# Moving one working tile behind the others, and the sums and x pieces of a three-stage network on one Trainium2 core

## The chip, the cores and the metric

The kernel runs on one core of one Trainium2 chip. The metric is the time of one execution on the device, in microseconds, as the median of several runs. TensorE (PE, with its weight loads PEld) multiplies out of SBUF into PSUM, VectorE (DVE), ScalarE (ACT) and GpSimd (POOL) work on SBUF and PSUM, and SyncE (SP) issues nearly all DMAs, in the order in which they are written.

## What is computed

Pooled attention over four batches of 576 tokens and eight heads makes x of 2304 x 512; a dense mixture of four experts follows, and a gated network with two more matrices. Everything is float32.

```python
k_p = k.reshape(B, H, Sp, 8, D).mean(axis=3)          # v_p likewise; Sp = 72
attn = softmax(q @ k_p.T / 8); x = attn @ v_p         # then laid out as 2304 x 512

p = domain_probs / (domain_probs.sum(-1, keepdims=True) + 1e-09)
for e in range(4):                                    # w1[e]: 512 x 1024, w2[e]: 1024 x 512
    out += p[:, e:e+1] * (np.maximum(x @ w1[e], 0.0) @ w2[e])

a = x @ w1; b = x @ w2                                # 512 x 1024 each
h = a * b @ w3                                        # 1024 x 1024
return h @ w_out                                      # 1024 x 512
```

## The kernel before

**Precision.** Every large product runs in the 4-byte type float32r, those of the attention stage in float32. An operand is split into a high part (a ScalarE copy) and a low part (the difference, by VectorE or GpSimd), `hi_lo`, lines 176 to 178; `mm3`, lines 171 to 174, issues three matmuls for one product: high x low, low x high, high x high. Each matmul brings its own weight load of 128 x 128 values; the moving operand has 384 or 512 columns.

**Order.** The whole program is written by hand in the order in which each engine runs it. The stages are: attention for six blocks of 384 tokens, woven into expert 0; experts 1 to 3 in batches of 768 tokens (`batch`, three batches an expert); w3 times w_out, folded into one matrix (`w3_h`, units "w"); the gated network in two halves of three batches each (from line 1329).

**A batch of 768 tokens.** The first layer of experts 1 to 3 and of the gated stage goes by `seven`: four rounds j, each with seven products of 2 x 3 matmuls of 384 columns, thus 168 matmuls (tile "s"). VectorE adds the seven results up (line 952) into the tiles x, u, v and c. The second layer of an expert then takes 6 token tiles x 8 x 3 = 144 matmuls of 512 columns (tile "g"), in the gated stage 6 x 4 x 3 = 72. Banks of PSUM go round in a ring of eight (`bank_r`). During an expert's second layer, the dictionary `acts` puts other work at numbered places, one place for each three matmuls.

**Sums.** What the experts add up lies in DRAM (`acc_d`). `load_ob(m)` (line 1182) fetches the sum of one token tile, and `give(m)` adds the expert's part (line 1242) and stores it or, for the last expert, turns it. In an expert's last batch the six sums lie at places that `ob_place` names: rows 2 and 3 of "plain", a place in x5l, then rows 0, 1 and 2 of "plain", fetched at places 14, 15, 16, 33, 34 and 40. Rows 0 and 1 of "plain" also hold the sums of the next expert's weights (`weights_of`, places 5 to 23).

**Rounding.** The 8-byte inputs of the gated network are brought to 4 bytes by `Rounding.step`, five VectorE operations and one GpSimd operation (lines 284 to 290), with three places for incoming data ("din", in x5h); a step fetches the data of the steps that follow (`load`), up to `most` steps in all.

**x for the gated stage.** Its seven products need x, its high and low parts, and four sums of them. `load_x` (line 774) fetches a half of x for the next batch, `prepare_x` makes the parts. The first operand (kc = 0) goes in three lumps behind the products j = 0, 1 and 2, the second one (kc = 1) in one lump behind the fourth product. Results of the second layer go out of PSUM by ScalarE (line 1395) into one of the four tiles of `rawpool` and are stored (line 1396). x's parts are stored too, for the second half (`put_away`, line 913).

**Places in SBUF.** Four pools follow each other: const, w2pool (the split w2 tiles, later w34), rawpool, and home. In the built program w2pool begins at byte 17,024 = 133 x 128, and home at 57,984 = 453 x 128. In home come first "plain", then "round" (the hidden values z and, later, w_out, called wo), "ap1" (later "xo", the x operands) and twelve tiles of 6,144 bytes (the split weights wh, wl, wx, z7 and others). All are multiples of 128 bytes but one:

```python
    WORK = 320
    PLAIN = WORK + XT + 3072          # XT = 6144: 9,536 bytes = 74.5 x 128
    plain = area("plain", PLAIN, F32, "plain")
    round_ = area("round", (FC - 1) * ZT + 2 * EXTRA, F32R, "round")
```

So every tile of home behind "plain" starts 64 bytes past a multiple of 128, and w2pool's tiles start at one. The matmuls of an expert's second layer read w2 as the moving operand (w2pool) and z as the stationary one (home); those of `seven` read xo and the split weights, both in home; those with wo read wo and w3, both in home.

## Time and profile before

| | |
|---|---|
| median of 3 runs | 1180.4 us (1179.27 to 1181.14) |
| the profiled execution's own time | 1179.82 us |
| its span, first to last instruction | 1177.7 us |
| PE busy | 1155.6 us, 98% of the span |
| DVE, POOL, ACT busy | 800.6, 421.0, 369.6 us |
| DMA | 213.85 MB, mean share of the 16 engines 59% |

A matmul's end is modelled and matmuls overlap, so PE's busy time tells whether it stands still, not how fast it goes. The pace is read from the starts of matmuls that follow each other, or from a stretch of known content divided by its number of matmuls.

### The profile page before, as it was taken

The page shows a single profiled execution, that of the slowest core. Times are in us where ns is not written, and L with a number is a line of the kernel's source. Part 1 is how long each engine was busy: PE and PEld are TensorE (multiplying, and loading weights), DVE is VectorE, ACT ScalarE, POOL GpSimd, SP SyncE. Part 2 cuts the span into 40 slices and gives each one's busy share as a digit, 9 for nine tenths or more (in the row PEclk, how much of TensorE's full clock was granted, in tenths as well). Part 3 has the DMA queues.
Part 4 walks back from the last instruction along what each step waited for, and adds up shares of the span by engine and source line. Part 5 has one row for each costly group of instructions (what it writes and reads, how often), then busy time and mean ns, then how long its engine had stood idle before and what let it go on. Part 6 is the DMA issues. An engine that isn't in the chain of part 4 may idle for free.

```text
span 1177.7 us, 17100 instructions
## 1 busy us (share of the span) xinstructions
PE 1155.6 (98%) x5966; PEld 1033.6 (88%) x5966; DVE 800.6 (68%) x1464; ACT 369.6 (31%) x615; POOL 421.0 (36%) x393
## 2 busy tenths in 40 slices
PE   8999999999999999999999899999999999999998
PEld 6788888989889898889898798989889898998997
DVE  6866553577768696658679486967677766774554
ACT  4543442344313152404134241405343313230100
POOL 6965213333525166534436371515000111331211
PEclk9999999999999999999999999999999999999999
DMA  8956514364966636295944568784476064946341
GB/s 210 212 145 142 168 68 161 147 208 166 312 220 205 213 85 191 82 312 168 269 148 131 176 201 201 215 225 119 157 180 251 28 268 171 337 166 253 130 167 54
DMA packets 213766, 213.85 MB, mean 182 GB/s; under 512 B 88880, under 2 KB 169008, under 8 KB 213680
## 3 DMA queue, kind: packets, MB, share of 16 engines
q1 hardware_dynamic: 213392, 212.23, 58.1%
q8 instruction: 47, 0.77, 0.3%
q10 hardware_dynamic: 288, 0.52, 0.1%
q14 instruction: 39, 0.32, 0.1%
HBM read 140.87 MB, written 71.83 MB: 181 GB/s over the span
## 4 chain that ended last, share of the span: by engine, by line
PE 76%; DVE 9%; issue 6%; DMA 4%; POOL 3%; ACT 1%; SPq 1%; POOLq 0%; DVEq 0%; ACTq 0%
PE g L173 15%; PE g L172 14%; PE g L174 14%; PE s L172 9%; PE s L174 9%; PE s L173 9%; PE x_ps L556 1%; PE sc L502 1%; DVE wl L178 1%; DVE plain L952 1%; PE at_ps L541 1%; DMA raw<-in_moe_w_dram 1%; POOL round L178 1%; POOL w2l L178 1%; DMA acc<-plain 1%
## 5 line engine op out<-in xcount | busy, mean ns | idle before, releaser
L172 PE MATMUL s<-xo,wh 128*128 128x384 f32 x624 | 209.7, 336 | 7.1 <-DVE plain L1242 7.1
L178 POOL TENSOR_TENSOR round<-x5l,round 128x768 fp32r<-128x768 f32 x60 | 112.2, 1871 | 278.2 <-ACT round L177 259.3
L952 DVE TENSOR_TENSOR plain<-s,plain 128x384 f32<-128x384 f32 x300 | 157.9, 554 | 78.2 <-ACT plain L956 37.6
L174 PE MATMUL s<-xo,wh 128*128 128x384 f32 x624 | 209.2, 335 | 0.0
L173 PE MATMUL s<-xo,wl 128*128 128x384 f32 x624 | 209.2, 335 | 0.0
L172 PE MATMUL g<-w2l,round 128*128 128x512 f32 x522 | 207.3, 397 | 0.0
L173 PE MATMUL g<-w2h,round 128*128 128x512 f32 x522 | 206.6, 396 | 0.0
L174 PE MATMUL g<-w2h,round 128*128 128x512 f32 x522 | 206.2, 395 | 0.0
L172 PEld LDWEIGHTS s<-xo,wh 128*128 128x128 f32 x624 | 117.7, 189 | 9.3 <-issue 4.6
L174 PEld LDWEIGHTS g<-w2h,round 128*128 128x128 f32 x522 | 98.1, 188 | 23.3
L173 PEld LDWEIGHTS s<-xo,wl 128*128 128x128 f32 x624 | 117.6, 188 | 0.6
L174 PEld LDWEIGHTS s<-xo,wh 128*128 128x128 f32 x624 | 117.6, 188 | 0.0
L172 PEld LDWEIGHTS g<-w2l,round 128*128 128x128 f32 x522 | 98.2, 188 | 21.8 <-issue 0.8
L173 PEld LDWEIGHTS g<-w2h,round 128*128 128x128 f32 x522 | 98.1, 188 | 21.3
L956 ACT ACTIVATE plain<-s 128x384 f32<-128x384 f32 x60 | 29.1, 484 | 258.0 <-PE s L174 232.3
L290 POOL TENSOR_TENSOR x5l<-x5l,x5h 128x256 uint32<-128x256 uint32 x80 | 60.6, 758 | 137.8 <-DVE x5h L289 130.0
L178 POOL TENSOR_TENSOR round<-plain,round 128x768 fp32r<-128x768 f32 (+1 forms) x29 | 51.9, 1791 | 134.2 <-ACT round L177 93.7
L177 ACT ACTIVATE round<-x5l 128x768 fp32r<-128x768 f32 x60 | 50.8, 847 | 152.5 <-DVE x5l L1325 151.3
L284 DVE TENSOR_SCALAR x5l<-x5h 128x256 uint32<-128x256 uint32 x80 | 57.4, 718 | 51.3 <-DMA gate<-x5l 28.7
L952 DVE TENSOR_TENSOR x5l<-s,plain 128x384 f32<-128x384 f32 x120 | 64.8, 555 | 23.4 <-PE s L174 15.7
L688 DVE SCALAR_TENSOR_TENSOR round<-g,round 128x384 fp32r<-128x384 f32 x48 | 26.6, 554 | 68.0 <-ACT round L687 67.9
L172 PE MATMUL g<-xl,round 128*128 128x384 f32 x192 | 66.4, 346 | 1.2 <-DVE round L688 1.2
(229 smaller groups left out, 2213.5 us busy)
## 6 DMA issues: line engine op xcount, KB each, us to landing
xo<-keptx SPq DMA_DIRECT2D x42, 768.0 KB
raw<-in_moe_w_dram SPq DMA_DIRECT2D x64, 256.0 KB
keptx<-xo SPq DMA_DIRECT2D x12, 768.0 KB
x5h<-in_moe_w_dram SPq DMA_DIRECT2D x128, 64.0 KB
x5h<-in_moe_w_dram SPq DMA_DIRECT2D x32, 256.0 KB
ob<-acc SPq DMA_DIRECT2D x24, 256.0 KB
kept<-xo SPq DMA_DIRECT2D x8, 768.0 KB
xo<-kept SPq DMA_DIRECT2D x8, 768.0 KB
```

The costliest lines, as they stand in the source:

```text
L172: nc.tensor.matmul(ps, lh, rl, start=first, stop=False)
L173: nc.tensor.matmul(ps, ll, rh, start=False, stop=False)
L174: nc.tensor.matmul(ps, lh, rh, start=False, stop=last)
L177: nc.scalar.activation(hi, src, AF.Copy)
L178: (lo_eng or nc.vector).tensor_tensor(lo, src, hi.bitcast(F32), op=ALU.subtract)
L284: nc.vector.tensor_scalar(au, h, 0x7FFFFFFF, None, op0=ALU.bitwise_and)
L290: nc.gpsimd.tensor_tensor(au, au, l, op=ALU.add)
L502: nc.tensor.matmul(sc[off:off + n, (hp % 2) * W:(hp % 2 + 1) * W], qT[:, hp, off:off + n], kT_t[b][:, hp * W:(hp + 1) * W], start=True, st ...
L541: nc.tensor.transpose(pt[:NK, g * P:(g + 1) * P], e[:, half * G + g, :], ident)
L688: nc.vector.scalar_tensor_tensor(hl, ps, 0.0, hh.bitcast(F32), op0=ALU.max, op1=ALU.subtract)
L952: nc.vector.tensor_tensor(to, one, two, op=ALU.add)
L956: nc.scalar.activation(x, product(j, A11, B11), AF.Copy)
```

## The change

"plain" leaves home for a pool of its own, opened behind it; home's other tiles all move down by 9,536 bytes, to multiples of 128. An expert's last batch keeps its sums 3 to 5 in x5h, at the rounding's places, and fetches them at places 24, 25 and 26; the rounding takes its last four steps there at places 2, 7, 12 and 17, and fetches nothing beyond them. `prepare_x` has five pieces instead of three. Two of the gated results go to two new places in "plain". Six numbers that say when x's sums are made in expert 0 move by one or two places.

```diff
+    work = ctx.enter_context(tc.tile_pool(name="work", bufs=1))
...
-    plain = area("plain", PLAIN, F32, "plain")
+    plain = work.tile([P, PLAIN // 4], F32, tag="plain", name="plain")
...
-            late["gated"] = dict(xr=Ring(x5[0], [0]), s=Ring(x5[0], [0]), half=row(x5[0], 0, ROW, 2), c=c_ring,
+            late["gated"] = dict(xr=Ring(x5[0], [0]), s=Ring(x5[0], [0]), half=row(x5[0], 0, ROW, 2), c=c_ring, early=row(plain, WORK, ROW, 2),
...
-                return Ring(x5[1], [C1]) if m == 2 else Ring(plain, [WORK + (2, 3, 0, 0, 1, 2)[m] * ROW])
+                return Ring(x5[1], [C1]) if m == 2 else Ring(plain, [WORK + (m + 2) * ROW]) if m < 2 else Ring(x5[0], [(m - 3) * ROW])
...
-            if n in (None, 0):
+            if n == 0:
                 r = sums_t[kc] = xr_t.pop(kc)
-                hi_lo(bh[:, 0], bl[:, 0], r[:, 0, 0])
-                hi_lo(bh[:, 1:], bl[:, 1:], r[:, 1])
-            if n in (None, 1):
-                make_sums(sums_t[kc])
-            if n in (None, 2):
+                nc.scalar.activation(bh[:, 0], r[:, 0, 0], AF.Copy)
+                nc.scalar.activation(bh[:, 1:], r[:, 1], AF.Copy)
+            if n == 1:
+                r = sums_t[kc]
+                nc.vector.tensor_tensor(bl[:, 0], r[:, 0, 0], bh[:, 0].bitcast(F32), op=ALU.subtract)
+                nc.vector.tensor_tensor(bl[:, 1:], r[:, 1], bh[:, 1:].bitcast(F32), op=ALU.subtract)
+            if n in (2, 3):
+                make_sums(sums_t[kc], n - 2)
+            if n == 4:
...
-        for (b, kc), begin, base in zip(((b, kc) for b in order for kc in range(2)), (56, 62, 68, 74, 82, 89), homes):
+        for (b, kc), begin, base in zip(((b, kc) for b in order for kc in range(2)), (56, 62, 67, 72, 80, 90), homes):
...
-        at_pairs = {39: 0, 43: 1, 47: 2}
-        also.setdefault(2 * 39, []).append(enter_weights)
+        at_pairs = {38: 0, 43: 1, 47: 2}
+        also.setdefault(2 * 38, []).append(enter_weights)
...
+                if j == 3 and last and not end:
+                    rounding.most = rounding.steps + 4
...
-                for m, at in enumerate((14, 15, 16, 33, 34, 40)):
+                for m, at in enumerate((14, 15, 16, 24, 25, 26)):
                     act(at, lambda m=m: load_ob(m))
...
-                    act(2 + 6 * i, lambda: round_some(1))
+                    act(2 + 5 * i, lambda: round_some(1))
...
-                    for i in range(3):
-                        act(12 + 12 * kc + 4 * i, lambda kc=kc, i=i: prepare_x(kc, first_x[kc], kept_d[g_order[0]][kc], i))
+                    for i in range(5):
+                        act(11 + 12 * kc + 2 * i, lambda kc=kc, i=i: prepare_x(kc, first_x[kc], kept_d[g_order[0]][kc], i))
...
-                    if j < 3:
-                        next_x(0, spare_slot, j)
-                    elif make:
-                        load_x(nb, 1)
+                    if make:
+                        prepare_x(0, spare_slot, kept_d[nb][0], j)
+                    elif j == 0 and not last:
+                        fetch_x(0, spare_slot, kept_d[nb][0])
...
-                next_x(1, first)
+                if make:
+                    prepare_x(0, spare_slot, kept_d[nb][0], 4)
+                    load_x(nb, 1)
+                elif not last:
+                    fetch_x(1, first, kept_d[nb][1])
...
+                    elif m < 2:
+                        ob = late["small"].tile([P, DM], F32, tag="early", name="ob")
...
-                if half == 0 and n_b < BN - 2:
-                    load_x(g_order[n_b + 2], 0)
                 for m in range(2 if last else len(tiles)):
                     run(m, range(NJ - 1))
+                    if make and m >= 3:
+                        for n in ((0, 1), (2, 3), (4,))[m - 3]:
+                            prepare_x(1, first, kept_d[nb][1], n)
...
+                if half == 0 and n_b < BN - 2:
+                    load_x(g_order[n_b + 2], 0)
```

PE's and GpSimd's instructions stand in the same order before and after. On SyncE, in the last batch of expert 1 (acc is the sums in DRAM, raw the weights of expert 2), there stood:

```order
L1187 DMA x5l<-acc 128x512
L196 DMA raw<-in_moe_w_dram 128x512 x2
L259 DMA x5h<-in_moe_w_dram 32x512 x4
L724 DMA gate_102<-x5l 128x2x128
L196 DMA raw<-in_moe_w_dram 128x512 x6
L1187 DMA plain<-acc 128x512 x2
L1244 DMA acc<-plain 128x512 x2
L1187 DMA plain<-acc 128x512
L1244 DMA acc<-x5l 128x512
L1244 DMA acc<-plain 128x512 x3
L264 DMA x5h<-in_moe_w_dram 128x2x256
```

And after the change there stands at the same place of SyncE:

```order
L1192 DMA x5l<-acc 128x512
L197 DMA raw<-in_moe_w_dram 128x512 x2
L725 DMA gate_105<-x5l 128x2x128
L197 DMA raw<-in_moe_w_dram 128x512 x2
L1192 DMA x5h<-acc 128x512 x2
L197 DMA raw<-in_moe_w_dram 128x512
L1192 DMA x5h<-acc 128x512
L197 DMA raw<-in_moe_w_dram 128x512 x3
L1251 DMA acc<-plain 128x512 x2
L1251 DMA acc<-x5l 128x512
L1251 DMA acc<-x5h 128x512 x3
L265 DMA x5h<-in_moe_w_dram 128x2x256
```

The last three sum loads move ahead of three or four of the six weight loads, and the rounding's next loads move behind the stores of the sums. On VectorE, in the first gated batch, the fourth product and what follows it stood so (L952 adds a product's results, L1325 multiplies the two halves, L836 to L840 make x's sums, L178 subtracts the high part):

```order
L1325 TENSOR_TENSOR x5l<-x5l,plain 128x768
L836 TENSOR_TENSOR x5h<-x5h 128x384
L837 TENSOR_TENSOR x5h<-x5h 128x384
L839 TENSOR_TENSOR x5h<-x5h 128x384
L840 TENSOR_TENSOR x5h<-x5h 128x384
L952 TENSOR_TENSOR plain<-s_8217,plain 128x384
L952 TENSOR_TENSOR plain<-s_8225,plain 128x384
```

And after the change, from the same multiplication on:

```order
L1332 TENSOR_TENSOR x5l<-x5l,plain 128x768
L837 TENSOR_TENSOR x5h<-x5h 128x384
L838 TENSOR_TENSOR x5h<-x5h 128x384
L957 TENSOR_TENSOR plain<-s_8278,plain 128x384
L957 TENSOR_TENSOR plain<-s_8286,plain 128x384
L957 TENSOR_TENSOR plain<-s_8294,plain 128x384
L957 TENSOR_TENSOR plain<-s_8302,plain 128x384 x2
L957 TENSOR_TENSOR x5l<-s_8311,plain 128x384
L957 TENSOR_TENSOR x5l<-s_8319,plain 128x384
L1332 TENSOR_TENSOR x5l<-x5l,plain 128x768
L840 TENSOR_TENSOR x5h<-x5h 128x384
L841 TENSOR_TENSOR x5h<-x5h 128x384
```

Two of the four sums now stand behind the fourth product instead of between the second and the third; the first operand's last subtraction follows them.

## Rows read from the trace of the kernel before

**Rows 1.** The page: TensorE's busy time (share, instructions), and VectorE's adds (busy, mean ns).

```profile
PE 1155.6 (98%) x5966; PEld 1033.6 (88%) x5966; DVE 800.6 (68%) x1464; ACT 369.6 (31%) x615; POOL 421.0 (36%) x393
...
L952 DVE TENSOR_TENSOR plain<-s,plain 128x384 f32<-128x384 f32 x300 | 157.9, 554 | 78.2 <-ACT plain L956 37.6
```

**Rows 2.** Waits of TensorE: engine and line, waited for: us in total, times, longest.

```profile
PE s L172 <- DVE plain L1242: 7.1, 4, 2.5
...
PE g L172 <- DVE round L688: 1.2, 1, 1.2
```

**Rows 3.** Windows: us, each engine's busy us (instructions), clock, DMA share, GB/s.

```profile
30.00:100.00 70.00, 67.16 (x409) 58.44 (x409) 50.39 (x97) 32.57 (x67) 49.34 (x77) 1.00 0.79 185
339.87:369.00 29.13, 29.13 (x169) 29.13 (x168) 23.70 (x44) 12.98 (x18) 13.24 (x9) 1.00 0.46 147
369.00:402.60 33.60, 33.60 (x146) 27.08 (x146) 23.13 (x55) 2.22 (x3) 10.63 (x11) 1.00 0.89 273
465.32:499.72 34.40, 31.50 (x169) 30.60 (x168) 19.43 (x35) 13.95 (x20) 17.73 (x13) 0.95 0.35 106
658.77:692.70 33.93, 29.68 (x169) 29.05 (x168) 17.83 (x32) 13.92 (x20) 17.27 (x13) 1.00 0.46 151
941.84:973.39 31.55, 29.71 (x170) 29.07 (x168) 19.83 (x30) 6.18 (x11) 3.89 (x3) 1.00 0.64 250
```

**Rows 4.** Windows, TensorE on tile s alone (all of 384 columns): us, busy us (instructions).

```profile
0.00:1178.00 1178.00, 442.91 (x2520) 1.00 0.59 182
```

**Rows 5.** The same on tile g (384, 512 and, at the end, 256 columns).

```profile
0.00:1178.00 1178.00, 659.92 (x2940) 1.00 0.59 182
```

**Rows 6.** Groups by shape, one of three lines each: expert 0's first layer; moving wo.

```profile
L172 PE MATMUL g<-xl,round 128*128 128x384 f32 x192 | 66.4, 346 | 1.2 <-DVE round L688 1.2
...
L172 PE MATMUL g<-round 128*128 128x512 f32 x56 | 21.8, 389 | 0.0
```

**Rows 7.** Timeline of TensorE (start, us): first matmul on wo, and the 46th.

```profile
851.75 0.40 PE L172 MATMUL g<-round 128*128 128x512 f32 x1
...
861.97 0.39 PE L172 MATMUL g<-round 128*128 128x512 f32 x1
```

**Rows 8.** Timeline of TensorE: first and last of the 24 matmuls of 256 columns.

```profile
1171.62 0.28 PE L172 MATMUL g<-w34l,round 128*128 128x256 f32 x1
...
1174.23 0.28 PE L174 MATMUL g<-w34h,round 128*128 128x256 f32 x1
```

**Rows 9.** Timeline of TensorE in the attention stage: 4-byte matmuls of 192 and 128 columns.

```profile
16.85 2.77 PE L450 MATMUL vp_ps<-stxl,ident 72*72 72x192 f32 x16
19.45 0.82 PE L631 MATMUL warm<-ident 128*128 128x128 f32 x6
20.11 1.04 PE L541 MATMUL at_ps<-ident,ap 128*72 128x128 f32 x8
```

**Rows 10.** Timeline of SyncE's queue, last batch of expert 1 (start, us of issuing).

```profile
458.90 8.08 SPq L196 DMA_DIRECT2D raw<-in_moe_w_dram  x6
...
471.95 0.32 SPq L1187 DMA_DIRECT2D plain<-acc  x1
```

**Rows 11.** Timeline of VectorE there: start, us, and in brackets the wait before.

```profile
475.06 0.75 DVE L1242 SCALAR_TENSOR_TENSOR plain<-g,plain 128x512 f32<-128x512 f32 x1 [2.94 <-DMA plain<-acc]
```

**Rows 12.** Timeline of VectorE and of GpSimd in expert 0.

```profile
257.34 4.32 DVE L178 TENSOR_TENSOR wl<-raw,wh 128x512 fp32r<-128x512 f32 x2
...
257.10 4.29 POOL L829 TENSOR_TENSOR s<-xh,xl 128x768 f32<-128x768 f32 x2
```

**Rows 13.** Timeline of ScalarE at the end of the first gated batch.

```profile
948.62 1.09 ACT L1395 ACTIVATE ob<-g 128x512 f32<-128x512 f32 x2 [7.39 <-DMA half<-ob]
```

**Rows 14.** Timeline there: load of x's second half, ScalarE's and VectorE's last pieces.

```profile
926.75 0.80 SPq L774 DMA_DIRECT2D x5h<-turned  x2
...
937.80 1.49 ACT L177 ACTIVATE xo<-x5h 128x1536 fp32r<-128x1536 f32 x1 [4.41 <-DVE x5h L840]
...
939.32 1.76 DVE L178 TENSOR_TENSOR xo<-x5h,xo 128x1536 fp32r<-128x1536 f32 x1 [1.56 <-ACT xo L177]
```

More of the change, by code (lines that the diff above doesn't have):

```diff
@@ L1208, in batch @@
                     late["small"].rings["s"] = Ring(plain, [WORK])
+                if j == 1:
                     rounding.most = STEPS
-                if j == 1:
                     rounding.load()
+                if j == 3 and last and not end:
+                    rounding.most = rounding.steps + 4
                 if j == 2 and last and not end:
@@ L1335, in fused_kernel @@
                 make = half == 0 and not swap
-                def next_x(kc, to, n=None):
-                    if make:
-                        prepare_x(kc, to, kept_d[nb][kc], n)
-                    elif not last and n in (None, 0):
-                        fetch_x(kc, to, kept_d[nb][kc])
                 for j in range(NJ):
```

## The prediction

> **What bounds the kernel now.** The page's busy table comes first: TensorE is busy 98% of the span [rows 1], far ahead of any other engine. So time can leave in two ways only: the engine's idle stretches shrink, or the same matmuls take less time each. The view of TensorE's waits prices the first: the largest entry is 7.1 us, behind VectorE's line 1242 [rows 2], and the busy table leaves only 1177.7 - 1155.6 = 22 us of idle time in all. For the second I cut the span at the blocks that the code gives: 168 matmuls of 384 columns for one batch's seven products times four, 144 of 512 columns for its second layer. The windows show both without a gap [rows 3]: 29.13 us / 168 = **173.4 ns** and 33.60 us / 144 = **233.3 ns**. The granted clock there is 1.00, the 2.4 GHz level, at which one column a cycle would be 160.0 and 213.3 ns. Every matmul thus loses 13 to 20 ns, and there are 2520 + 2940 of them [rows 4, 5]: this is the large sum, and the question is whether operand offsets cause it.
>
> **What the rows say of offsets.** From the kernel: w2 and w34 tiles start at multiples of 128 bytes (offset 0 below); every tile behind "plain" starts 64 past one (offset 64), thus every stationary operand of these matmuls, and the moving x and wo. In cycles of 2.4 GHz: 384 columns, moving 64, stationary 64: 173.4 ns = 416, so 32 more than columns. 512 columns, 64 and 64: 45 matmuls between 851.75 and 861.97, 227.1 ns [rows 7] = 545, again 32 to 33 more. 512 columns, moving 0, stationary 64: 560, so 48 more. 256 columns, 0 and 64: 23 steps in 2.61 us, 113.5 ns [rows 8] = 272, so 16 more. Same instruction, same 512 columns, and the pace changes by 6 ns at 851.75 when wo takes the place of w2: placement does matter to the pace. The swap of weights alone does not cost 32 cycles: the attention stage's 4-byte matmuls, which run at two cycles a column, swap weights each time too and take 2.60 us / 16 = 162.5 ns for 192 columns (160.0 + 2.5) and 0.66 us / 6 = 110 ns for 128 (106.7 + 3.3) [rows 9]. I take 2.6 ns as what is left of a swap. The reading that fits best: an operand 64 bytes off touches one more 128-byte length than it fills, and 32 columns of 4 bytes are 128 bytes: (12 + 1) x 32 = 416 cycles = 173.3 ns, (16 + 1) x 32 = 544 = 226.7 ns, both as measured. The mixed pair adds conflicts of its own (16 at 256 columns, 48 at 512).
>
> **The change, part by part.**
> *Offsets.* "plain" goes behind "home", so every large matmul's operands, moving and stationary, come to offset 0. TensorE's instructions stay the same in number and order. By the reading above each takes columns / 2.4 + 2.6 ns: 162.6 for 384, 215.9 for 512. 384 columns: 2520 + 3 x 192 = 3096 [rows 4, 6] x 10.8 ns = 33.4 us. 512 columns: 2940 - 576 - 24 = 2340; of these 3 x 56 = 168 had both operands at 64 [rows 6]: 168 x 11.2 = 1.9 us; the other 2172 x 17.4 = 37.8 us. Sum **73.1 us**, all on the path, since TensorE is the path. No row shows a pair at 0 and 0 in these matmuls, so the bounds: at most bare columns / 2.4, another 5436 x 2.6 ns = 14 us; at least nothing. A loss is bounded too: if the moving operand's offset alone counts, and 0 is the slow one, 16 more at 256 and 48 more at 512 put 384 at 32 more, where it is, and only the 168 lose 6 ns each, 1 us. I take the 73, nearest to rows 9 and to the exact 32 in rows 3 and 7.
>
> The Trainium skill speaks against this edit: "SBUF — State Buffer" (Door 1: The DMA port swizzle) gives SBUF lines of 16 bytes, by which offset 64 already starts a line and the edit would return 0; row 851.75 disagrees, as the pace there changes with the place alone. Its page "TensorE: Matmul & The Clock Gate" (Back-to-back issue gap) gives columns / 2.4 + 2.5 ns, 162.5 and 215.8, by which the sum would be 73.6; no row of the large matmuls reaches that.
>
> *Sums of the last batch.* Blocks that follow the last batch of experts 1 and 2 take 34.40 and 33.93 us instead of 29.13 [rows 3]: 5.27 + 4.80 = 10.07 us lost. The chain: SyncE takes 8.08 us over six weight loads, issues the sum loads only behind them, the last at 471.95 [rows 10]; VectorE's line 1242 waits 2.94 us for that one [rows 11]; TensorE has no free bank. Inside it the clock falls to 0.95 of full on the mean [rows 3], which is in the 5.27. After the change the three loads go to the rounding's places, which are free once the batch's four rounding steps are done (no more than four are loaded), and stand ahead of all but one of those weight loads. SyncE may now wait for the rounding step itself, with weight loads of the next expert queued behind it; VectorE works that step off some 10 us before the block ends, so I keep 0.25 us a block: **-9.6 us** (bounds -10.1 and 0).
>
> *Earlier preparation in expert 0.* GpSimd's two adds of x (4.29 us) lie on top of VectorE's two subtractions, which took 4.32 us for two [rows 12], and TensorE then waits 1.2 us on line 688 [rows 2]. One place earlier or later in each pair keeps them apart: **-1.2 us** (bounds -1.4, +1).
>
> *Gated stage.* The first gated batch's successor takes 31.55 us, 2.42 over 29.13 [rows 3]. Half of this is ScalarE waiting 7.39 us for a store, since the fifth output needs the first one's buffer [rows 13]; two more buffers end that. The other half is VectorE working x's pieces in one lump; they are now spread over the four products. New is a longer chain. The second operand's load goes out when the first operand's last subtraction is done. Now that is at 926.75, 1.7 us into the second layer (which begins 72 x 0.233 = 16.8 us before 941.84), and from there to the second operand's end it is 14.3 us (926.75 to 941.08) [rows 14]. After the change the first operand's last piece stands behind the fourth product: three adds and two sums of 0.554 us each [rows 1], 2.8, and a split of 3.3 (937.80 to 941.08) [rows 14], 6.1 us at most instead of 1.7. So 16.0 to 20.4 us, against a second layer of 72 x 215.9 ns = 15.5 plus one product, 1.0: a wait of 0 to 3.9 us in each of two batches. I take 2.0 each: -2.4 + 4.0 = **+1.6 us** (bounds -2.4, +5.4).
>
> *What is late next.* With TensorE 6 to 7% faster, VectorE's 23.70 us in a 29.13 us block stand against 27.3: 87%, still covered. From 30 to 100 us the DMA share is 0.79 and VectorE and GpSimd are busy 50.4 and 49.3 of 70 us [rows 3]; there some of the gain will be given back. I put **+4 us** (0 to 10) for it and for the second layers, and keep both ends.
>
> Sum against the profiled execution's 1179.8 us (span 1177.7 and 2.1 around it): 1179.8 - 73.1 - 9.6 - 1.2 + 1.6 + 4.0 = 1101.5. The median of the three runs is 0.6 higher: **1102 us**. Its own range: down to 1088 with half of the 14 us below the 2.6 ns and no new waits in the gated stage or elsewhere; up to 1130 if the conflicts shrink only by half, or if the terms above all end at their poor side and VectorE gives more back.
>
> **The rivals.**
> *The offsets only have to be equal.* Then 0 and 0 behaves as 64 and 64: 384 columns keep 173.4, and the 2172 mixed ones go from 233.3 to 227 ns: 14 us. For it: equal offsets give 32 at both sizes. Against it: 256 columns at unequal offsets lose only 16, less than that supposed floor. With the waits (-9.6 - 1.2 - 0.9, as the slower second layer lets the chain lag by less): 1179.8 - 25.7 = 1154, and up to 1166 if the waits come back elsewhere.
> *Offsets do nothing.* The pace at 851.75 changed for another reason. Only the waits go: 1168 (1179.8 - 9.6 - 1.2 - 0.9), or no change if they are merely renamed. The Trainium skill's 16-byte lines ("SBUF — State Buffer", Door 1: The DMA port swizzle) lead to this case.
> *Slower.* Offsets return nothing, the sum loads stay late behind the weight load that is still ahead of the last of them, and the gated chain decides: 20.4 - (16.8 + 1.0) = 2.6 us in each of two batches, against 2.4 removed: +2.8, so 1183 us beside the median of 1180.4. It decides only if offsets, sum loads and the preparation in expert 0 together return less than 2.8 us.
>
> **How the numbers follow.** Full effect of the offsets: 0.58, 1102. Equal offsets: 0.22, 1154 to 1166. Nothing from offsets: 0.13, of which 0.08 with the waits gone (1168) and 0.05 with them renamed. Slower: 0.07. The range from 1088 to 1166 leaves out the last two, 0.20. Within 0.2% is about what a measurement of this kernel can tell from no change. Faster: 0.58 + 0.22 + 0.08 = 0.88; same 0.05; slower 0.07.
>
> **What would show it.** Right: a block of 168 takes 27.3 us and one of 144 takes 31.1; the steps of 256 columns come down towards 109 ns; line 1242 is gone from TensorE's waits; the two long blocks are as short as their neighbours. The equal-offset rival: 29.1 and 32.6 to 32.7 us. Offsets idle: both blocks as they were. The gated chain shows as a wait of TensorE near the second product of the second and third gated batch. I am wrong if a stationary operand at 0 meets the moving one in conflicts that no row here shows, or if VectorE, not TensorE, ends most blocks.

## The result and the profile after

The changed kernel takes **1164.4 us** (median of four runs, 1163.9 to 1165.4) against 1179.8 for the kernel before on the same chip: a ratio of 0.987, interval 0.985 to 0.989. The gain is 15.5 us. 78 had been forecast, and the time lies at the far end of the range from 1088 to 1166. The profiled execution took 1164.6 us, its span is 1162.9, 14.8 less than before.

The page of the kernel after: busy times, and VectorE's adds, as in [rows 1].

```profile
PE 1144.2 (98%) x5966; PEld 1035.3 (89%) x5966; DVE 792.1 (68%) x1464; ACT 370.0 (32%) x615; POOL 423.5 (36%) x393
...
L957 DVE TENSOR_TENSOR plain<-s,plain 128x384 f32<-128x384 f32 x300 | 158.2, 554 | 90.6 <-ACT plain L961 39.3
```

TensorE's busy time fell by 11.4 us only, for the same 5966 instructions; VectorE's adds take the same 554 ns each. Next, TensorE's waits in the kernel after, the first of the list (engine and line, waited for: us in total, times, longest):

```profile
PE s L173 <- ACT plain L961: 7.7, 1, 7.7
```

The two entries of [rows 2] are gone: VectorE's sums (then line 1242) and the split in expert 0 (then line 688). A single wait of 7.7 us has come instead, on ScalarE's copy of a gated product. Windows of the kernel after, with the columns of [rows 3] (us, each engine's busy us and instructions, clock, DMA share, GB/s):

```profile
336.79:365.94 29.15, 29.15 (x170) 29.15 (x169) 23.76 (x44) 12.95 (x18) 13.30 (x9) 1.00 0.47 147
365.94:398.62 32.68, 32.68 (x146) 27.03 (x146) 22.99 (x55) 2.25 (x3) 10.63 (x11) 1.00 0.90 270
460.44:489.59 29.15, 29.15 (x170) 29.14 (x168) 19.03 (x35) 13.80 (x20) 18.68 (x13) 1.00 0.43 133
645.92:675.07 29.15, 29.15 (x170) 29.14 (x168) 18.51 (x33) 13.86 (x21) 19.05 (x13) 1.00 0.55 182
904.73:921.10 16.37, 16.37 (x74) 13.53 (x74) 8.50 (x12) 5.65 (x7) 1.86 (x1) 1.00 0.14 48
921.10:960.52 39.42, 31.76 (x169) 31.44 (x168) 20.71 (x35) 7.90 (x15) 5.72 (x3) 0.87 0.52 200
940.00:950.00 10.00, 5.45 (x18) 5.45 (x19) 5.23 (x10) 2.39 (x4) 0.00 (x0) 0.52 0.20 77
```

Read against [rows 3]: a block of 168 matmuls of 384 columns takes what it took, 29.15 us, 173.5 ns each. A block of 144 of 512 columns went from 33.60 to 32.68 us, 233.3 to 227 ns. The two long blocks are short (34.40 and 33.93 to 29.15 each). The block after the first gated batch went from 31.55 to 39.42 us, and the granted clock falls in it: 0.52 from 940 to 950, near the 1.2 GHz level, behind TensorE's wait of 7.7 us. The 24 matmuls of 256 columns at the end answer [rows 8]; they now take 2.75 us for 23 steps, 120 ns, where it was 113.5:

```profile
1156.64 0.28 PE L173 MATMUL g<-w34l,round 128*128 128x256 f32 x1
...
1159.39 0.28 PE L175 MATMUL g<-w34h,round 128*128 128x256 f32 x1
```

**Where the time went.** Worked out from the starts of blocks in the two traces: 8 second layers of 144 x 0.92 = -7.4; w_out's block of 336 -0.9; the second layers of 72, 6 x 0.44 = -2.6; the two long blocks -5.25 - 4.78 = -10.0; expert 0's last 447 matmuls -1.4; the stage up to 185 us -0.8; the gated block +7.9. Sum -15.2, beside -14.8 of the spans; the twelve other blocks of 384 columns and the last 24 matmuls give +0.3. The -0.8 is no finding: that stage ends at 184.95 us here and at 184.04 in a run below whose code is the same up to there. So the waits came out nearly as forecast, the offsets returned some 11 us instead of 73, and a wait that the prediction didn't have took 8 back.

### The profile page after: what moved, and what is told of

Its sections match the earlier page's. It is cut to its first block, busy times and chain, and to the rows that moved or that the text cites. A ratio compares the mean times of both kernels' runs of the same rounds, so it can differ in the third digit from the quotient of the medians.

```text
span 1162.9 us, 17117 instructions
## 1 busy us (share of the span) xinstructions
PE 1144.2 (98%) x5966; PEld 1035.3 (89%) x5966; DVE 792.1 (68%) x1464; ACT 370.0 (32%) x615; POOL 423.5 (36%) x393
## 4 chain that ended last, share of the span: by engine, by line
PE 90%; issue 3%; DMA 3%; DVE 2%; SPq 1%; ACT 1%; POOL 1%; POOLq 0%; DVEq 0%; ACTq 0%
PE g L174 17%; PE g L175 17%; PE g L173 17%; PE s L173 12%; PE s L175 12%; PE s L174 12%; PE x_ps L557 1%; PE sc L503 1%; DMA raw<-in_moe_w_dram 1%; PE at_ps L542 1%; POOL round L179 0%; DMA x5h<-turned 0%; SPq L1403 0%; DVE ap L418 0%; DMA plain<-gate 0%
## 5 line engine op out<-in xcount | busy, mean ns | idle before, releaser
L173 PE MATMUL g<-w2l,round 128*128 128x512 f32 x522 | 204.4, 392 | 0.0
L175 PE MATMUL g<-w2h,round 128*128 128x512 f32 x522 | 204.1, 391 | 0.0
L174 PE MATMUL g<-w2h,round 128*128 128x512 f32 x522 | 203.9, 391 | 0.0
L178 ACT ACTIVATE round<-x5l 128x768 fp32r<-128x768 f32 x60 | 50.9, 848 | 146.1 <-DVE x5l L1332 145.0
L285 DVE TENSOR_SCALAR x5l<-x5h 128x256 uint32<-128x256 uint32 x80 | 50.5, 632 | 54.7 <-DMA gate<-x5l 31.1
```

The lines of the kernel that those rows point to most:

```text
L173: nc.tensor.matmul(ps, lh, rl, start=first, stop=False)
L174: nc.tensor.matmul(ps, ll, rh, start=False, stop=False)
L175: nc.tensor.matmul(ps, lh, rh, start=False, stop=last)
L178: nc.scalar.activation(hi, src, AF.Copy)
L285: nc.vector.tensor_scalar(au, h, 0x7FFFFFFF, None, op0=ALU.bitwise_and)
```

## Experiments: what each part is worth

**The offsets alone.** In the kernel before, "plain" alone moves into a pool of its own behind "home":

```
+    work = ctx.enter_context(tc.tile_pool(name="work", bufs=1))
-    plain = area("plain", PLAIN, F32, "plain")
+    plain = work.tile([P, PLAIN // 4], F32, tag="plain", name="plain")
```

> The kernel before with one edit: "plain" moves behind the other areas, so that every large matmul has both operands at multiples of 128 bytes. All order edits are left out. Theory A (only equality of the two offsets counts): the 512-column matmuls go from 233.3 to 227.0 ns and the 384-column ones stay at 173.5, so about 2172 x 6.3 ns = 14 us less, near 1166 us; blocks of 168 stay at 29.15 us, blocks of 144 fall to 32.7, and the two long blocks of 34.4 and 33.9 us and the wait of expert 0 are still there. Theory B (my prediction: an operand at a multiple of 128 loses nothing): 73 us less, near 1107, blocks of 168 at 27.3 us. Theory C (offsets do nothing, the order edits made the gain): near 1180.

Measured: 1170.4 us, ratio 0.992 (0.991 to 0.994), 9.3 us less. Windows of this kernel: a second layer, the second long block, and the block after the first gated batch.

```profile
306.14:338.83 32.69, 32.69 (x146) 27.05 (x146) 21.80 (x53) 3.28 (x4) 11.40 (x11) 1.00 0.93 305
653.01:688.49 35.48, 32.26 (x169) 31.24 (x168) 19.41 (x34) 14.06 (x21) 18.98 (x13) 0.90 0.46 151
934.33:966.85 32.52, 29.76 (x169) 29.09 (x168) 19.82 (x30) 6.29 (x11) 3.89 (x3) 1.00 0.63 243
```

Theory A holds for the blocks: 32.69 us, and nothing for 384 columns. Its time, near 1166, was missed by 4 us. The windows show 2.5 of them: the block at 653 takes 35.48 us (33.93 before) and the one at 934 32.52 (31.55). Where VectorE or a store ends a block, a faster TensorE only waits longer. Expert 0 holds back as much: it has 432 of the 2172 mixed matmuls, 2.7 us at 6.3 ns each. Its last 447 matmuls, groups of nine with 512 columns (207 in all) between groups of twelve with 384, took 91.39 us before and 91.51 here: in such short groups equal offsets returned nothing.

**The order alone.** The changed kernel with "plain" back in front (the same three lines, the other way).

> The changed kernel with "plain" put back in front of the other areas, so that every operand is 64 bytes past a multiple of 128 again; all order edits stay. Theory A (offsets return 14 us, the order edits nearly cancel): the two long blocks return 10.1 us, expert 0 1.3, and the new wait in the second gated batch costs 8, so about -3 us, near 1177. Theory C (offsets do nothing): near 1164, as the changed kernel. The new wait of some 7.8 us in the second gated batch should be there in both.

Measured: 1174.7 us, ratio 0.996 (0.994 to 0.997), 5.0 us less than before, where theory A had 3; from the end of the attention stage on, this trace is 3.8 us shorter than that of before. The first of TensorE's waits is the new one, without any change of offsets:

```profile
PE s L172 <- ACT plain L960: 7.7, 1, 7.7
```

Theory C is out. The parts sum to 14.3 us against 15.5 for both together. The wait belongs to the order edits.

**The sums of the last batch undone**, in the version with the load first (next section, 1156.4 us): their places, the rounding's steps and the loads' places are those of before.

```
-                for m, at in enumerate((14, 15, 16, 24, 25, 26)):
+                for m, at in enumerate((14, 15, 16, 33, 34, 40)):
...
-                    act(2 + 5 * i, lambda: round_some(1))
+                    act(2 + 6 * i, lambda: round_some(1))
```

> The version with the load first (1156.4 us) with the sums of an expert's last batch as in the kernel before: their places, the order of the rounding's steps there and the loads at 33, 34 and 40 instead of 24, 25 and 26. If that part of the change is worth what the two long blocks lost (34.40 and 33.93 instead of 29.13 us, 10.1 in all), the time goes up by 9 to 11.5 us, to 1165.5 to 1168; with TensorE faster by 1 us in a second layer of 144 the wait could grow, as the block of 35.48 us in the run with the offsets alone has it. Rival (a third of it would be lost elsewhere anyway): 1162 to 1165.

Measured: 1168.5 us, 12.1 us more. The long blocks are back and a little longer than in [rows 3], as expected of a faster TensorE, and the clock falls in both:

```profile
460.13:496.17 36.04, 31.55 (x169) 30.62 (x168) 18.05 (x33) 13.97 (x20) 17.95 (x13) 0.95 0.33 102
652.51:687.36 34.85, 31.04 (x170) 30.23 (x168) 17.80 (x32) 13.93 (x20) 18.16 (x13) 0.95 0.50 153
```

So this part is worth 12 us once the others are in, a little more than the 9 to 11.5 expected and the most of all parts; the rival is out.

**The smaller pieces undone**, in the same version: the first operand in three pieces over three products, the second in one lump ahead of the second layer, as before. Buffers, loads and offsets stay.

```
-                        for n in ((0, 1), (2, 3), (4,))[m - 3]:
-                            prepare_x(1, first, kept_d[nb][1], n)
...
+                    for n in range(5):
+                        prepare_x(1, first, kept_d[nb][1], n)
```

> The version with the load first (1156.4 us) with the preparation of gated x as in the kernel before: the first operand in three pieces with the splits whole, the second in one lump between the fourth product and the second layer. The loads, the buffers of the outputs and the offsets stay as changed. If the smaller pieces do what I forecast, TensorE waits on VectorE again in the two batches that follow such a lump: 1 us as at 968.05 in the kernel before, or up to 1 in each of two, so 1157 to 1159. If the buffers of the outputs alone ended the 2.4 us, the time stays within 1 us of 1156.4.

Measured: 1156.0 us, the same as with the pieces. The first two gated blocks of that run:

```profile
920.86:950.70 29.84, 29.43 (x170) 29.11 (x169) 19.82 (x30) 6.00 (x11) 3.87 (x3) 1.00 0.68 265
...
967.34:996.48 29.14, 29.14 (x169) 29.14 (x168) 18.57 (x31) 6.18 (x12) 5.54 (x3) 1.00 0.94 355
```

0.7 us stays in the first of them, and with the pieces 1.3 us stays in the second (30.42). The smaller pieces return nothing that shows here. The offsets alone left 32.52 us in that block, so what ended the 2.42 us of [rows 3] is, by elimination, mostly the outputs' own buffers; no run changed these alone. Lumps in the fastest version below were not tried.

## Experiments: the new wait

Timeline of SyncE's queue in the kernel after (start, us of issuing, tiles), around the end of the first gated batch:

```profile
911.00 0.80 SPq L775 DMA_DIRECT2D x5h<-turned  x2
921.16 0.81 SPq L1403 DMA_DIRECT2D half<-plain  x2
922.02 2.17 SPq L918 DMA_DIRECT2D kept<-round  x3
924.23 1.55 SPq L918 DMA_DIRECT2D kept<-z  x1
925.82 5.54 SPq L918 DMA_DIRECT2D kept<-xo  x4
931.45 5.10 SPq L1403 DMA_DIRECT2D half<-ob  x4
936.60 2.40 SPq L775 DMA_DIRECT2D x5h<-turned  x2
```

The load at 911.00 is the second operand's, the one that the prediction watched. The one at 936.60 is the following batch's first operand; the change moved it behind the stores of the prepared x ("kept") and of the outputs ("half"). ScalarE and VectorE there (start, us, and in brackets the wait before and what ended it):

```profile
942.43 0.52 ACT L905 ACTIVATE xo<-x5h 128x384 fp32r<-128x384 f32 x1 [11.34 <-DMA x5h<-turned]
943.27 0.84 ACT L906 ACTIVATE xo<-x5h 128x768 fp32r<-128x768 f32 x1 [0.33 <-DMA x5h<-turned]
944.02 0.47 ACT L961 ACTIVATE plain<-s 128x384 f32<-128x384 f32 x1
...
944.53 2.81 DVE L957 TENSOR_TENSOR plain<-s,plain 128x384 f32<-128x384 f32 x5 [14.38 <-ACT plain L961]
```

The preparation's first piece stands behind the first product on ScalarE. It waits 11.34 us for that load; the copy of a product that stands behind it waits too, VectorE's adds wait for the copy, and TensorE has no free bank. The question is what makes the load late.

**Ahead of all the stores.** The statement moves from behind the outputs to the end of the loop that issues the second operand's pieces:

```
                         for n in ((0, 1), (2, 3), (4,))[m - 3]:
                             prepare_x(1, first, kept_d[nb][1], n)
+                if half == 0 and n_b < BN - 2:
+                    load_x(g_order[n_b + 2], 0)
```

> The changed kernel with one statement moved: the load of the next gated batch's first operand is issued ahead of the stores of the prepared x and of the outputs, once the second operand's pieces are issued, instead of behind all of them. Theory D (this load, queued behind the stores on SyncE, makes the new wait of 7.8 us): the load starts near 923 instead of 936.6 us, TensorE's wait on the first product's ScalarE copy goes and with it the stretch at half the clock, about 8 us less, near 1156. Rival E (the wait comes from the finer pieces themselves, which share ScalarE and VectorE with the products): the wait only changes its name, and the time stays within 2 us of 1164.

Measured: 1156.4 us, ratio 0.980 (0.979 to 0.982). The block takes 29.26 us at a clock of 1.00; 1.3 us comes up in the next one, where VectorE is late:

```profile
920.86:950.12 29.26, 29.26 (x170) 29.12 (x168) 18.84 (x32) 7.96 (x15) 5.71 (x3) 1.00 0.69 270
966.48:996.90 30.42, 29.42 (x170) 29.10 (x168) 19.33 (x31) 7.88 (x14) 5.54 (x3) 1.00 0.90 340
```

**Between the stores.** The same statement behind the stores of x, ahead of the last four stores of outputs (right behind `put_away()`).

> The changed kernel with the load of the next gated batch's first operand behind the stores of the prepared x, but ahead of the last four stores of the outputs. Theory D (the place of this load in SyncE's queue sets the wait, us for us): in the changed kernel it was issued at 936.6 us, and the output stores ahead of it took 5.2 us, so it starts near 931.5, the wait of 7.8 us falls to 0 to 3, and the time lies between 1156.4 and 1160. Rival (any load behind the stored x waits the same, since the DMA engines are full until 940): 1162 to 1164.

Measured: 1163.4 us: the rival is right. The load is issued 5.3 us earlier than in the changed kernel (SyncE's queue, then ScalarE's wait) and lands about half a microsecond earlier:

```profile
931.26 2.52 SPq L775 DMA_DIRECT2D x5h<-turned  x2
...
941.88 0.52 ACT L905 ACTIVATE xo<-x5h 128x384 fp32r<-128x384 f32 x1 [10.93 <-DMA x5h<-turned]
```

The window of the 12 us ahead shows the DMA engines full, at 408 GB/s:

```profile
924.00:936.00 12.00, 12.00 (x71) 12.00 (x70) 4.70 (x8) 0.85 (x1) 1.85 (x1) 1.00 1.03 408
```

So the place in SyncE's queue alone isn't the price; what is ahead in the DMA engines may be. The stored x is 5.5 MB (the sizes of its eight issues: 4 x 768 and 4 x 576 KB), some 13.5 us at 408 GB/s. The next run tests this.

**The stored x behind the load.** The changed kernel with `put_away()` moved from behind the second output to behind the load, so that only the six output stores (1.5 MB) are ahead of it.

```
-                    if m == 1:
-                        put_away()
...
                 if half == 0 and n_b < BN - 2:
                     load_x(g_order[n_b + 2], 0)
+                put_away()
```

> The changed kernel with the stores of the prepared x (8 of them, about 5 MB) behind the load of the next first operand, while the six stores of outputs (1.5 MB) stay ahead of it. The last run that moved the load past four output stores only gained 1 us, with the DMA engines at a share of 1.0 and some 410 GB/s from 924 to 938 us. Theory N (what the load waits for is the bytes ahead of it in the DMA engines, above all the prepared x): the load is issued near 924 to 925 us, TensorE's wait of 7.8 us goes, and the time is 1156 to 1157.5 us. Rival (the output stores ahead of it, or the load's own length, matter as much): part of the wait stays, 1159 to 1164.

Measured: **1153.9 us**, ratio 0.979 (0.977 to 0.980), the fastest of all. SyncE's queue and ScalarE:

```profile
921.11 2.10 SPq L1403 DMA_DIRECT2D half<-ob  x4
923.31 1.65 SPq L775 DMA_DIRECT2D x5h<-turned  x2
...
929.92 0.51 ACT L905 ACTIVATE xo<-x5h 128x384 fp32r<-128x384 f32 x1
```

The block's window:

```profile
919.99:949.17 29.18, 29.18 (x170) 29.12 (x168) 21.11 (x35) 7.77 (x15) 5.72 (x3) 1.00 0.71 271
```

The piece at 929.92 shows no wait, and the block at 965.53 takes 29.18 us as well. Theory N holds, with 10.5 us, more than the load ahead of all stores returned, and 2 us under its own range: of the 2.2 us between those two traces 0.8 lie in the attention stage, where the kernels are the same, and 1.2 in the block that took 30.42. Whether the bytes of the stored x count or the number of its packets was not tried.

Issuing the four output stores takes 2.10 us here, near the head of the stores, and 5.10 in the changed kernel, behind ten other stores. The DMA share was 1.04 and 1.02 meanwhile, so the share alone doesn't set it. In the changed kernel the first four stores took 0.32 to 0.44 us each to issue, and from the fifth on each took 1.1 to 1.7, whether of 256 or of 768 KB.

## Experiments: what an operand's offset costs

The three rows of matmuls in this section ran once each; a block repeats its matmul 32 times.

**All pairs, mixed.** A row of matmuls alone, moving tiles 2304 bytes apart, weights 640.

> Not the computation but a row of matmuls alone (every other part is left out, and the output is one of their results, repeated): float32r, blocks of 32 with new weights for each, over pairs of offsets of the moving and the stationary operand past a multiple of 128 bytes, for 512, 384 and 256 columns, then with 96, 64 and 32 columns of weights, and with the same weights throughout. Theory A (equal offsets): 32 columns more wherever the two are equal, whatever they are, so 545, 416 and 288 cycles of 2.4 GHz, and 48 more at 512 or 16 more at 256 where they are 64 apart. Theory F (the 32 columns are the reading of the next weights, 128 columns x 4 bytes = 32 lines of 16): the loss goes down to 24, 16 and 8 columns with 96, 64 and 32 columns of weights. Theory B (length of 128 bytes touched in excess): the loss doesn't depend on the weights' width, and offsets 0 and 0 give none; the changed kernel already speaks against it.

Windows over blocks of 32 matmuls of 512 columns (the first value behind the window is its length; divide by 32): offsets 0/0; moving 0, weights 64; 0/0 with 64 and with 32 columns of weights; the same weights throughout at 0/0, and at 0/64.

```profile
30.66:38.10 7.44, 7.44 (x34) 6.01 (x32) 0.00 (x0) 0.00 (x0) 0.00 (x0) 1.00 0.00 0
45.52:53.00 7.48, 7.48 (x34) 6.03 (x32) 0.00 (x0) 0.00 (x0) 0.00 (x0) 1.00 0.00 0
...
266.01:273.30 7.29, 7.29 (x35) 4.28 (x33) 0.00 (x0) 0.00 (x0) 0.00 (x0) 1.00 0.00 0
299.34:306.70 7.36, 7.36 (x34) 3.47 (x32) 0.00 (x0) 0.00 (x0) 0.00 (x0) 1.00 0.00 0
332.61:339.89 7.28, 7.28 (x34) 6.02 (x33) 0.00 (x0) 0.00 (x0) 0.00 (x0) 1.00 0.00 0
339.89:347.36 7.47, 7.47 (x34) 6.02 (x32) 0.00 (x0) 0.00 (x0) 0.00 (x0) 1.00 0.00 0
```

With changing weights 0/0 took 232.5 ns, hardly less than 0/64 (233.8): theory A fails as it was put. With the same weights they differ as in the kernels, 227.5 and 233.4. Narrower weights (7.29 and 7.36 us) don't bring the loss down in step: theory F is out. No block of 512 came below 227, so theory B gets nothing either.

**At a fixed distance modulo 512.** The same with tiles 2048 and 512 bytes apart, as they lie in the kernel.

> Again a row of matmuls alone (nothing else is computed), but now the moving tiles lie 2048 bytes apart and the weights 512, as in the kernel, so that a pair keeps its distance modulo 512 through a block; the distance of weights from moving operand goes through 16 values from 0 to 496. In the last row of matmuls, with tiles 2304 and 640 bytes apart, 512 columns took 231 to 233 ns at every pair, and 227.4 ns only with the same weights throughout. Theory A2 (the distance of the two operands decides, and that row mixed several): 227 ns at distance 0 and 233 at 64, constant within a block, and other distances tell whether any loses less than 32 columns. Rival G (changing weights cost the 6 ns, not the distance): 231 to 233 at all distances. Theory B (multiples of 128): the distances of 128, 256 and 384 as good as 0, and (64, 64) worse than (0, 0).

Windows over 32 matmuls each: 512 columns, weights 64 bytes further than the moving operand; 192 further; both at 192; 384 columns, distance 0 and 64; 256 columns, distance 0 and 64.

```profile
58.59:66.04 7.45, 7.45 (x33) 6.01 (x32) 0.00 (x0) 0.00 (x0) 0.00 (x0) 1.00 0.00 0
88.44:95.78 7.34, 7.34 (x34) 6.01 (x33) 0.00 (x0) 0.00 (x0) 0.00 (x0) 1.00 0.00 0
169.54:176.81 7.27, 7.27 (x33) 6.01 (x32) 0.00 (x0) 0.00 (x0) 0.00 (x0) 1.00 0.00 0
176.81:182.36 5.55, 5.55 (x33) 5.54 (x32) 0.00 (x0) 0.00 (x0) 0.00 (x0) 1.00 0.00 0
199.03:204.58 5.55, 5.55 (x33) 5.55 (x33) 0.00 (x0) 0.00 (x0) 0.00 (x0) 1.00 0.00 0
288.51:292.35 3.84, 3.84 (x34) 3.84 (x34) 0.00 (x0) 0.00 (x0) 0.00 (x0) 1.00 0.00 0
303.69:307.33 3.64, 3.64 (x34) 3.64 (x33) 0.00 (x0) 0.00 (x0) 0.00 (x0) 1.00 0.00 0
```

Theory A2 holds for 512 columns: the distance decides. For 512 columns, steps inside the blocks: 226.7 to 227 ns at 0, 16, 256 and 496; 229 at 192 and 448 (each 64 short of a multiple of 256); 232 to 234 at all others. 384 columns: 173.3 at 0 to 96, 192, 256, 448 and 496, 176 to 177 at the rest. 256 columns: 113.3 at 64, and 117 to 120 elsewhere, 120.0 at 0. The distance isn't quite all: (64, 128) gave 176.7 at 384 columns and 117.8 at 256, where (0, 64) gave 173.3 and 113.3. At 512 columns 128 and 384 are worse than 0, and (64, 64) and (192, 192) as good as (0, 0): theory B is out, and so is rival G. The kernels' own 233.3, 227.0, 173.4, 113.5 and 120 ns are all in this table. No distance gets 512 or 384 columns under 32 columns of loss. The table doesn't give the mixed row, though: there 0/64 goes through the distances 64, 448, 320 and 192, whose mean is 231.1 ns in this table, and took 233.8; 0/0 goes through 0, 384, 256 and 128, 229.6 in the table, and took 232.5. How neighbours at different distances act on each other was not tried; expert 0's short groups may be such a case.

**Both at 64, in the kernel.** The version with the load first, with 64 bytes ahead of w2 (and 32 fewer at the front of "plain", to make room).

```
+    front = ctx.enter_context(tc.tile_pool(name="front", bufs=1))
+    front.tile([P, 16], F32, tag="front", name="front")
```

> The version with the load first (1156.4 us), with 64 bytes put in front of all large areas, so that the moving and the stationary operands of every large matmul stand 64 bytes past a multiple of 128. Theory A (only equality counts): the same time, within 2 us of 1156, and blocks of 144 at 32.7 us. Theory H (0 is better than 64 for its own sake): 512 columns back at 233 ns, 14 us more, near 1170.

Measured: 1157.1 us beside 1156.4, the same. A block of 144 takes 32.68 us:

```profile
306.88:339.56 32.68, 32.68 (x145) 27.04 (x145) 21.73 (x53) 3.28 (x4) 10.87 (x11) 1.00 0.93 302
```

That an offset is a multiple of 128 bytes is worth nothing for its own sake.

**The other way round.** "home" ahead of w2, with the 64 bytes between them and the same 32 fewer in "plain": moving operand at 64, weights at 0.

> The version with the load first (1156.4 us), with w2 and w34 now 64 bytes past a multiple of 128 and everything else at one, so that the moving operand of the second layers is at 64 and the stationary at 0, the reverse of the kernel before. Theory A (only equality counts, the sign of the distance doesn't matter): 512 columns at 233 ns, 13.5 us more, near 1170. Rival (only the stationary operand's offset matters): 227 ns, as 1156. From the first row of matmuls alone, where this pair took 231.0 and the other 233.3 ns, something between, 1164, is possible.

Measured: 1158.8 us, 2.4 more, and 32.96 us for a block of 144, so 228.9 ns:

```profile
303.75:336.71 32.96, 32.96 (x145) 27.04 (x145) 22.07 (x53) 3.27 (x4) 10.98 (x11) 1.00 0.92 302
```

That is neither of the two theories. The sign of the distance matters, as the table above has it (229 with the weights 64 bytes behind).

**What the 32 columns are.**

> A row of matmuls alone (nothing else is computed), all at distance 0, to see what the 32 columns are that no distance of the operands took away (512 columns: 545 cycles of 2.4 GHz at best, 384: 416, 256: 272 to 288, while 192 and 128 columns both took 268). Theory K (a share of the moving operand's reading, one line in so many): the loss grows with the columns, and 320 to 448 columns lie on a line through 416 and 545. Theory L (a fixed cost of the weights' change, one for each matmul): 32 more at every size above 256, and the same weights again change nothing because they are loaded again. Theory M (it depends on the bank or on the moving tile changing): one bank or one moving tile for all lose less. Bfloat16 operands (half the bytes) and float32 (two cycles a column in the attention part: 2.6 to 3.3 ns over the columns) tell whether four-byte reading at a column a cycle is the condition.

Windows over 32 matmuls of 128 columns of weights, distance 0: float32r of 384 and of 512 columns; then bfloat16 of 512 and of 384.

```profile
50.32:55.87 5.55, 5.55 (x34) 5.55 (x33) 0.00 (x0) 0.00 (x0) 0.00 (x0) 1.00 0.00 0
75.44:82.74 7.30, 7.30 (x34) 5.93 (x32) 0.00 (x0) 0.00 (x0) 0.00 (x0) 1.00 0.00 0
...
159.69:166.60 6.91, 6.91 (x33) 3.14 (x33) 0.00 (x0) 0.00 (x0) 0.00 (x0) 1.00 0.01 2
166.60:171.80 5.20, 5.20 (x33) 3.13 (x32) 0.00 (x0) 0.00 (x0) 0.00 (x0) 1.00 0.00 0
```

Bfloat16 takes 215.9 and 162.5 ns, that is columns / 2.4 + 2.5: the price that the prediction had for everything. Float32r takes 227 to 228 and 173.4. One bank for all, one moving tile, the same weights, half the rows: all 226.7 to 227.5 at 512, so theory M is out. 320 and 352 columns lose 32, 448 lose 48, 480 40 and 512 32 to 34: neither a share of the columns nor quite a fixed cost, so theories K and L both fit badly. 128, 192 and 224 columns all take 111.7 ns with 128 columns of weights; with 32 columns of weights 128 take 60.0 and 192 take 88.3, so there the weights set the pace. Float32, two cycles a column, takes 215.8 ns a step of 256 columns, 2.5 over, as bfloat16 does. So the loss of 32 columns was seen with float32r at a column a cycle alone, and no placement tried here takes it away. What in the chip makes it stays open.

## Why the prediction was wrong

*What bounds the kernel*: right. TensorE is 98% busy before and after, and what the changes returned was on its path.

*The offsets, 73.1 us*: this is the step that failed. Two readings carried it. First, the swap of weights was priced at 2.6 ns by [rows 9], float32 matmuls at two cycles a column, and this was carried to float32r at one. Bfloat16 agrees with that price, float32r at distance 0 doesn't: 226.7 instead of 215.8 ns at 512, 173.3 instead of 162.5 at 384. Second, the 32 columns were read as one more 128-byte length, touched by an operand 64 bytes off. That explanation was made to fit two numbers ([rows 3, 7]) and none of the rows had a pair at 0 and 0. It also needed a special clause for 256 columns at unequal offsets, which lose only 16 [rows 8]. The prediction used these 16 against the rival of equal offsets ("less than that supposed floor"); in truth 256 columns are the size at which a distance of 64 is the best, and the kernel after has them at 120 ns. The rival's own price, 14 us for 2172 matmuls, is what came, less the 2.7 us of expert 0: in blocks it is 11, and 9.3 alone, where waits take some back. The likeliest case should have been the one with a row in the trace: a pair at equal offsets was seen at 227.1 ns [rows 7], a pair without loss was seen nowhere. That the time still lies inside the range is luck: 1166 was the upper end of the rival, for waits that come back elsewhere, and the one that came was on a load that the prediction didn't price. Without that wait the kernel took 1153.9 to 1156.4 us, near the rival's 1154.

The Trainium skill, "TensorE: Matmul & The Clock Gate" (Back-to-back issue gap), gives columns / 2.4 + 2.5 ns as the isolated gap of a matmul. By the bfloat16 blocks (6.91 us / 32 = 215.9 ns) the trace agrees; by the float32r blocks (7.30 / 32 = 228.1, with steps of 226.7 inside) it doesn't, and the page doesn't part the two. The same page of the Trainium skill (Step-by-step: what each phase is for) has the weights read through a port of their own, without taking bandwidth from the running matmul. Here the pace of 512 columns went from 226.7 to 233.3 ns with nothing but the distance between the two operands changed, so for float32r the pace is not free of where the weights lie; how the two readings meet in the chip, if they do, no run shows.

*Sums of the last batch, -9.6*: right. Both blocks are 29.15 us, -10.0, and the undone version shows 12.1 beside a faster TensorE. The 0.25 us that were kept for SyncE's wait on the rounding did not come.

*Expert 0, -1.2*: right; the wait of 1.2 us is gone, and the 447 matmuls there take 90.01 us instead of 91.39 (89.87 with the order edits alone).

*Gated stage, +1.6*: the sign was right, the step wrong. The chain that was priced behaves as worked out: the second operand's load goes out at 911.00, 6.3 us into the second layer, which begins at 904.73 (6.1 at most forecast), and its last split is this one on VectorE:

```profile
920.68 1.76 DVE L179 TENSOR_TENSOR xo<-x5h,xo 128x1536 fp32r<-128x1536 f32 x1 [1.56 <-ACT xo L178]
```

It ends 17.7 us after the layer's start (16.0 to 20.4). No wait comes of it. What was left out is the other load that the diff moves, the next batch's first operand, past eight stores of x and six of outputs on SyncE; its wait made the block 7.9 us longer than before. Two lines of the diff showed that move, and the transfer's 5.5 MB could have been priced: [rows 3] show 250 GB/s at a DMA share of 0.64 in this very block, so some 390 with the engines full and 14 us for them. The forecast place, "near the second product of the second and third gated batch", was right for the second by accident: TensorE stops after 90 of 168 matmuls, in the third of four rounds, but on the other load, and in one batch only, as only one batch has such a load. And the smaller pieces, priced at half of the 2.4 us, are worth nothing that shows.

*Late next, +4*: mis-sized and misplaced. The stage up to 185 us lost nothing that shows. What a faster TensorE gives back shows where another engine ends a block: 1.55 and 0.97 us in the run with the offsets alone.

## What to carry to other kernels

When a cost per instruction is to vanish, look for a row in which the same type of operand already runs without it; if there is none, the best pace that the trace shows for that type is the forecast, and the clean one a rival. When a load is moved behind stores, count the bytes of those stores against the DMA rate, not the instructions in the queue: here 5.5 MB ahead of a 768 KB load cost 8 us, the wait moved by next to nothing when the load was issued 5.3 us earlier behind them, and went when the stores went behind. A wait long enough to drop the clock costs more than itself: 7.7 us of waiting made a block 10.3 us longer.

## What the runs showed of the hardware

- Float32r at a column a cycle never came below 32 columns of loss at 384 and 512 columns, while bfloat16 and float32 at two cycles a column lose about 6 cycles (215.9 ns for 512 columns in bfloat16, 215.8 for 256 in float32).
- In an unbroken row at one distance, the pace of float32r depends on how far the two operands lie apart, and on the columns: 512 took 227 ns at 0, 16, 256 and 496 bytes, 233 at 64 and 229 at 64 behind; 384 took 173.3 at 0 to 96; 256 did best with the moving operand at 0 and the weights at 64 (113.3; 120.0 at 0 and 0). Where groups of 9 and 12 alternate, equal offsets returned nothing (91.39 and 91.51 us).
- Behind a row of stores, SyncE's issuing slows: 0.32 to 0.44 us for each of the first four, 1.1 to 1.7 from the fifth on, whatever their size.
- TensorE waited 7.7 us up to 944.5, and the granted clock was 0.52 over 940 to 950.
